# New order numbers for the second part of a three-stage kernel, and three pieces of work placed behind others

## The chip, the cores and the metric

One core of a Trainium2 chip runs the whole program. Its engines are TensorE (PE in the profile; PEld is its loading of weights), VectorE (DVE), ScalarE (ACT), GpSimd (POOL) and SyncE (SP). The metric is the device time of one execution in microseconds (us), a median over runs; less is better.

## The reference

Three stages follow one another; the output of each is the input of the next.

```python
# 1. attention with random features; q, k, v: (8, 8, 576, 64), w_phi: (64, 128)
proj = einsum(x, w_phi); proj -= max(abs(proj))
phi  = concat(exp(proj), exp(-proj))
num / den = phi(q) @ (phi(k)^T v)  /  phi(q) . sum(phi(k))
# 2. 4608 tokens of 512, 8 experts of capacity 576
logits = x @ w_gate
for (token, expert) in descending order of logits:       # greedy
    if token is free and expert has room: assign
out[mask_e] = relu(x[mask_e] @ w1[e]) @ w2[e]             # 512 -> 1024 -> 512
# 3. on all tokens
h = x @ w_in                                              # 512 -> 2048
return (h - tanh(h)) @ w_out                              # 2048 -> 512
```

## The kernel before

The program is in two parts. The first, the attention with its own order numbers `AT`, ends at about 503 us and is not touched. The second is the function `ffn`. It takes the experts one after another, so that a token's whole way (both expert layers, then w_in, the function and w_out) is done while it is on the chip.

All matrices are held as two 16-bit numbers, a high part and the low rest, so each product of two matrices is three matmuls (high by high, high by low, low by high). "Splitting" a matrix is a scaling, a conversion to the high part and a subtraction that leaves the low part.

For expert p the parts are these; lines are those of the kernel before.

- `routing(p)`: the greedy choice. DVE makes integer keys from the logits (L843 multiplies and compares, L880 and L883 arrange, L846 and the last L843, an exclusive or, make the key). Then 16 steps of a search follow, each of which counts keys over three bounds: two counts on DVE (L898), one on ACT (L896), L846 takes ACT's, one small matmul (L902) sums over partitions, L904 compares, and L850 and L843 set the next bounds. The search for expert p+1 runs while expert p is computed; only the first stands alone.
- `xt(p)`: the tokens. POOL issues five indirect gathers (L1161). For expert 0 TensorE transposes them (L1169), for the others a DMA does, after ACT and DVE have split them (L1179, L1180).
- `wprep(p)`: the weights. POOL issues the gathers of w1 and w2 (L1097), ACT sums squares for the scale (L309), L1105 adds them up, and then each of the four pieces is split: w1 of expert 0, and both matrices of experts 2 to 7, by ACT and DVE (L1118, L1119); w2 of expert 0 and both matrices of expert 1 (the table `WPOOL`) by two passes of ACT and a subtraction on POOL (L1114, L1115, L1116).
- `g1(p)`: the first expert layer, 16 tiles of 128 x 288 results with 12 matmuls each (L1190, `mm<-xh,wt`). Each tile is drained by ACT's relu (L1203), copied to the high part (L1204) and its low part is made on POOL (L1205). There are three accumulators `mm` and three buffers `r`.
- `g2(p)`: the second expert layer, 8 tiles of 24 matmuls, drained by ACT (L1216) and DVE (L1217) into `y`. Then `scale_g(p)` finds the scale for what follows (L1233, L1237).
- `batch(p)`: 16 column groups f. For each, 12 matmuls with w_in (L1190, `mm<-gw,win`), then the function h - tanh(h) in pieces on ACT (L1315 to L1318, L1335) and DVE (L1324, L1325, L1327, L1328, L1336), whose result g is a pair of the ring of five, and 12 matmuls with w_out (L1342) that add into four accumulators `po`. At the end of a batch the four are evicted by ACT (L1353) into a ring of two buffers, and POOL scatters each to the output rows (L1357).
- a batch holds 512 of an expert's 576 tokens. The other 64 of each expert are put aside (`rest`) and make a ninth batch at the end of the program, with its own lines for the function (L1311 to L1313, L1321, L1322, L1331 to L1333).

Two things happen once, ahead of expert 0: `split64(1)` splits w_out in 16 chunks (ACT L763 and L764, POOL L765), and `scale_x` finds the scale of the tokens (L1128 to L1137, of which L1130 is the first step that needs data).

The order of instructions is made when the program is built. Each operation of `ffn` is handed to a list scheduler with its engine, an expected duration, the tiles it reads and writes, and a number, its priority (`pri`). The scheduler walks through time and gives each engine the ready operation with the lowest number. So the table `FT` is a table of due times: expert p has `expert`·p, its first layer's tiles come `g1` apart, its batch starts `tb` later with `step` per column group, the product with w_out is `lag` behind the product with w_in of the same group, and `sq`, `th`, `sq2`, `dv`, `dv2` and `gh` are the pieces of the function; `ev` is the evictions' offset from the end of the batch. What the chip sees of this is only the order on each engine; waits on the chip come from the data. An `after=` list, or a key that an operation reads without using its data, also acts on the order only.

## Time and profile before

| what | us |
|---|---|
| median of three runs | 1783.58 |
| the runs | 1783.58, 1779.04, 1784.16 |
| the profiled execution | 1777.59 |
| its span | 1775.8 |
| attention, to the first step of the first search | 503 |
| first matmul of expert 0 | 566.43 |
| last matmul of the program begins its row at | 1755.16 |
| busy in the span: PE, DVE, ACT, POOL | 1638.1, 1333.1, 1270.8, 515.9 |

A row of a timeline is one instruction or several of the same kind in a run: its start, how long it lasted, engine, line, operation, what is written <- what is read, shapes, and count. In square brackets stands how long the engine was idle before it, and whose end ended that. A row of waits has the waiting engine and tile, whom it waited for, the total time, how often, and the longest. PEclk is the granted TensorE clock as a share of full speed: 1.00 is the upper of its two levels, 2.4 GHz, and a stretch between 0.5 and 1.00 has run in part at 1.2 GHz. Names in the trace are those of a memory's first user: `gw` can be the attention's tile or what lies there later, as g of a batch.

### The profile page before, as it was taken

What the parts mean: (1) busy time and instruction counts of PE and PEld (TensorE: products, weight loads), DVE (VectorE), ACT (ScalarE), POOL (GpSimd) and SP (SyncE); (2) the same over time, 40 slices, a digit from 0 to 9 for tenths busy, and PEclk for the clock granted to TensorE, in tenths of its full rate; (3) what the DMA queues carried; (4) which work ended last, traced back from release to release, by engine and by line L of the source; (5) the groups of instructions that cost most, each with busy time, mean ns of one, the idle gap of its engine ahead of it and who ended that gap; (6) DMA issues with size and microseconds to landing.
All of it is one profiled execution on the core that took longest, in us unless ns stands there. A gap on an engine that the chain in (4) does not pass through costs nothing. (4 is left out here: it accounts for less than half of the span.)

```text
span 1775.8 us, 32280 instructions
## 1 busy us (share of the span) xinstructions
PE 1638.1 (92%) x11448; PEld 1066.1 (60%) x11448; DVE 1333.1 (75%) x4118; ACT 1270.8 (72%) x2513; POOL 515.9 (29%) x559
## 2 busy tenths in 40 slices
PE   6899999999935999999999999999999999999995
PEld 5888888888822744754754654664664664564442
DVE  6778888778878499589589689689679548436784
ACT  7787889877775679678678668668758658546653
POOL 3332245423043434432332332322322430210000
PEclk9999999889966999999999999999999999999998
DMA  8778776765503022022022022022113250000000
GB/s 202 171 183 190 185 168 153 160 169 142 140 19 115 11 84 63 28 84 69 25 84 65 25 79 71 28 67 76 32 61 83 63 107 13 25 1 1 18 7 24
DMA packets 230419, 145.95 MB, mean 82 GB/s; under 512 B 166080, under 2 KB 208960, under 8 KB 230256
## 3 DMA queue, kind: packets, MB, share of 16 engines
q1 hardware_dynamic: 214208, 90.25, 22.3%
q0 software_dynamic: 16048, 53.62, 9.4%
q8 instruction: 90, 1.47, 0.3%
q14 instruction: 73, 0.60, 0.1%
HBM read 89.16 MB, written 18.87 MB: 61 GB/s over the span
## 5 line engine op out<-in xcount | busy, mean ns | idle before, releaser
L1342 PE MATMUL po<-wout,gw 128*128 128x512 f16 x1728 | 401.3, 380 | 7.6 <-DVE gw L1336 3.9
L1190 PE MATMUL mm<-xh,wt 128*128 128x288 f16 x3072 | 392.2, 288 | 17.2 <-ACT r L1203 10.9
L1190 PE MATMUL mm<-gw,win 128*128 128x512 f16 x1728 | 397.2, 379 | 5.5 <-DVE gw L1217 3.0
L1190 PEld LDWEIGHTS <-wt 128*128 128x128 f16 x3072 | 296.1, 99 | 103.1 <-issue 17.4
L1342 PEld LDWEIGHTS <-gw 128*128 128x128 f16 x1728 | 164.3, 98 | 205.4 <-DVE gw L1336 11.4
L1190 PEld LDWEIGHTS <-win 128*128 128x128 f16 x1728 | 166.0, 98 | 199.3 <-issue 8.2
L1097 POOL DMA_INDIRECT wt<-moe_w,wrow x96 | 125.8, 1310 | 288.9 <-issue 148.4
L544 PE MATMUL bKV<-vp,kp 128*128 128x96 f32 (+1 forms) x1152 | 173.6, 290 | 3.6 <-ACT kvs L551 3.6
L570 PE MATMUL bN<-kvs,qt 128*128 128x96 f32 (+1 forms) x1152 | 158.1, 285 | 5.1 <-ACT qt L527 3.1
L1205 POOL TENSOR_TENSOR xh<-r,xh 128x288 f16<-128x288 f32 x128 | 95.7, 758 | 215.2 <-ACT xh L1204 214.1
L544 PEld LDWEIGHTS bKV<-vp,kp 128*128 128x128 f32 x1152 | 148.2, 197 | 12.9 <-POOL vp L450 4.2
L570 PEld LDWEIGHTS bN<-kvs,qt 128*128 128x128 f32 x1152 | 144.9, 198 | 8.3 <-ACT qt L527 3.3
L1335 ACT ACTIVATE gw<-s,sc 128x512 f16<-128x512 f32 x128 | 91.9, 718 | 53.4 <-DVE s L1328 46.3
L1315 ACT ACTIVATE u<-mm,sc 128x512 f32<-128x512 f32 x128 | 87.0, 679 | 58.4 <-PE mm L1190 57.4
L1336 DVE SCALAR_TENSOR_TENSOR gw<-s,sc,gw 128x512 f16<-128x512 f32 x128 | 98.1, 766 | 18.9 <-ACT gw L1335 18.4
L1324 DVE SCALAR_TENSOR_TENSOR u<-mm,sc,u 128x512 f32<-128x512 f32 x128 | 94.5, 741 | 20.2 <-ACT t L1316 17.2
L1328 DVE COPY_PREDICATED s<-mk,t 128x512 f32<-128x512 uint16 x144 | 105.5, 733 | 0.9
L1317 ACT ACTIVATE s<-u,cst 128x512 f32<-128x512 f32 x144 | 102.9, 714 | 1.3 <-DVE gw L1336 1.2
L1318 ACT ACTIVATE mk<-u,cst 128x512 f16<-128x512 f32 x144 | 102.4, 711 | 0.0
L1327 DVE SCALAR_TENSOR_TENSOR s<-s,u 128x512 f32<-128x512 f32 x144 | 99.9, 694 | 0.8
L904 DVE TENSOR_SCALAR_CACHE_REDUCE r_nn<-rtp,r_rem 128x7 f32<-128x7 f32 x112 | 24.9, 223 | 96.6 <-PE rtp L902 96.5
L1325 DVE SCALAR_TENSOR_TENSOR t<-mm,sc,t 128x512 f32<-128x512 f32 x128 | 94.7, 740 | 2.5 <-ACT t L1316 2.4
(312 smaller groups left out, 2905.6 us busy)
## 6 DMA issues: line engine op xcount, KB each, us to landing
rawk<-k SPq DMA_DIRECT2D x32, 256.0 KB, 3.5
rawv<-v SPq DMA_DIRECT2D x32, 256.0 KB, 3.5
gw<-moe_w_in SPq DMA_DIRECT2D x32, 256.0 KB, 3.2
gw<-moe_w_out SPq DMA_DIRECT2D x32, 256.0 KB, 3.1
rawq<-q SPq DMA_DIRECT2D x30, 256.0 KB, 3.9
xd<-X SPq DMA_DIRECT2D x32, 192.0 KB, 2.6
xd<-X SPq DMA_DIRECT2D x32, 64.0 KB, 2.4
wt<-moe_w,wrow POOLq DMA_INDIRECT x96, 4.2
```

The source lines that it names most:

```text
L544: mm(o, kp[:, c, a * NF:(a + 1) * NF], r, start=sl == 0 and a == 0, stop=sl == 8 and a == 1, skip_group_check=True)
L570: mm(o, qt[:, a, c], r, start=a == 0, stop=a == 1, skip_group_check=True)
L1097: S.pool(1040, lambda dst=dst, col=col, wf=wf: gp.indirect_dma_start(out=dst, out_offset=None, in_=wf, in_offset=bass.IndirectOffsetOnAxis ...
L1190: nc.tensor.matmul(pt.t[:, 0:un], wt(a, d), xs[hl][:, d, u0:u0 + un], start=d == 0 and a == 0 and hl == 0, stop=d == nb - 1 and a == 1)
L1205: S.pool(700, lambda r=r, f=f, u0=u0, un=un: gp.tensor_tensor(hl[:, f, u0:u0 + un], r, hh[:, f, u0:u0 + un], OP.subtract), [kr, f"h.{f}h{u ...
L1317: S.act(512, lambda u=u, s_=s_: act(s_, u, AF.Square, bias=cst[:, 0:1], scale=PC ** 0.5), [ku, "pa"], [ks], pri=tf + FT["sq2"])
L1318: S.act(512, lambda u=u, mk=mk: act(mk, u, AF.Relu, bias=cst[:, 8:9], scale=1024.0), [ku, "t2"], [km], pri=tf + FT["sq2"])
L1325: S.dve_s(512, lambda t=t, pt=pt, sc=sc: v.scalar_tensor_tensor(t, pt.t, sc[:, 0:1], t, op0=OP.mult, op1=OP.subtract), [pt, ksc, kt], [kt])
L1327: S.dve(512, lambda s_=s_, u=u: v.scalar_tensor_tensor(s_, s_, PC * PB, u, op0=OP.add, op1=OP.mult), [ks, ku], [ks], port=True)
L1328: S.dve(512, lambda s_=s_, mk=mk, t=t: v.copy_predicated(s_, mk.bitcast(U16), t), [ks, km, kt], [ks], port=True)
L1336: S.dve_s(512, lambda s_=s_, g=g, sc=sc: v.scalar_tensor_tensor(g[:, 1], s_, sc[:, 2:3], g[:, 0], op0=OP.mult, op1=OP.subtract), [ks, kgr ...
L1342: nc.tensor.matmul(outs[t].t, g[:, a, 128 * t:128 * t + 128], self.wout[:, w, f, :], start=f == 0 and k_ == 0, stop=f == 15 and k_ == 2)
```

## The change

The numbers of `FT` are new: 16 of its 24 entries. Three pieces of work get something to stand behind in the order. w_out's split (`split64(1)`) and the first step of the tokens' scale (L1130) are listed as readers of "r.key", which the search's key operation writes. The gathers of w2 for expert 0 come after the first tokens' gathers, which `xt` now collects in `came`. No instruction is added or removed, and all lines from L1154 on move down by up to three.

```diff
-FT = {'expert': 136.0, 'step': 5.3, 'lag': 11.0, 'route': 5.0, 'xt': -30.0, 'g1': 3.0, 'g2': 24.0, 'g2s': 6.0, 'sg': 49.0, 'tb': 50.0, 'w1': 30.0, 'w2': 40.0, 'rest': 10.0, 'ev': 8.0, 'tb8': 85.0, 'sq': 1.0, 'th': 1.2, 'sq2': 1.1, 'dv': 1.0, 'dv2': 2.0, 'gh': 3.0, 'h': 0.0, 'late': 1.2, 'room': 0.0}
+FT = {'expert': 136.0, 'step': 1.8, 'lag': 12.4, 'route': 5.0, 'xt': -30.0, 'g1': 2.5, 'g2': 21.1, 'g2s': 5.2, 'sg': 46.4, 'tb': 53.6, 'w1': 30.0, 'w2': 40.0, 'rest': 27.4, 'ev': -1.8, 'tb8': 64.6, 'sq': 1.0, 'th': 25.4, 'sq2': 3.4, 'dv': 20.9, 'dv2': 2.0, 'gh': 3.4, 'h': -3.3, 'late': 0.6, 'room': 0.0}
...
-    def split64(self, which, cw):
+    def split64(self, which, cw, after=()):
...
-            S.act(cw, lambda f=f, sc=sc: act(f, f, AF.Copy, scale=sc), [f"S64.{which}"], kf)
+            S.act(cw, lambda f=f, sc=sc: act(f, f, AF.Copy, scale=sc), [f"S64.{which}", *after], kf)
...
-            tt(JE, key, VT.bitcast(I32), key, OP.bitwise_xor, "VT wide", "wide")
+            tt(JE, key, VT.bitcast(I32), key, OP.bitwise_xor, "VT wide", "wide key")
...
-                            [kr], [kr_[c], kr_[c] + "h"], lat=4500)
+                            [kr], [kr_[c], kr_[c] + "h"], lat=4500, after=came if p == 0 and n else ())
...
-            S.dve(48, lambda: v.tensor_reduce(nx, self.ssx, axis=AX.X, op=OP.add), [], ["nx"])
+            S.dve(48, lambda: v.tensor_reduce(nx, self.ssx, axis=AX.X, op=OP.add), ["r.key"], ["nx"])
...
+        came = []
...
+            came.clear()
...
-                S.pool(1040, lambda x=x, m=m, t=t: gp.indirect_dma_start(
+                g = S.pool(1040, lambda x=x, m=m, t=t: gp.indirect_dma_start(
...
+                came.append(g)
...
-        split += self.split64(1, CW)
+        split += self.split64(1, CW, ["r.key"])
```

What the order becomes, at three places. First, on POOL at the start of the second part: L765 is w_out's split, L884 clears a tile of the search, L1097 are weight gathers (128x1024 of w1, 128x512 of w2), L1161 the tokens' gathers. Before:

```order
154 L765 TENSOR_TENSOR wout<-gw,wout 128x512 x2
155 L884 MEMSET r_V 128x288
156 L765 TENSOR_TENSOR wout<-gw,wout 128x512 x14
157 L1097 DMA wt<-moe_w,wrow_6308 128x1024 x4
158 L1097 DMA wt<-moe_w,wrow_6308 128x512 x3
159 L1161 DMA xg_6221<-xd,idx_6301 128x512
160 L1161 DMA xg_6222<-xd,idx_6301 128x512
161 L1161 DMA u_6227<-xd,idx_6301 128x512
162 L1161 DMA u_6228<-xd,idx_6301 128x512
163 L1161 DMA u_6229<-xd,idx_6301 128x512
164 L1097 DMA wt<-moe_w,wrow_6308 128x512 x3
165 L884 MEMSET r_V 128x288
```

and of the change:

```order
154 L884 MEMSET r_V 128x288
155 L765 TENSOR_TENSOR wout<-gw,wout 128x512 x16
156 L1097 DMA wt<-moe_w,wrow_6308 128x1024 x4
157 L1163 DMA xg_6221<-xd,idx_6301 128x512
158 L1163 DMA xg_6222<-xd,idx_6301 128x512
159 L1163 DMA u_6227<-xd,idx_6301 128x512
160 L1163 DMA u_6228<-xd,idx_6301 128x512
161 L1163 DMA u_6229<-xd,idx_6301 128x512
162 L884 MEMSET r_V 128x288
163 L1097 DMA wt<-moe_w,wrow_6308 128x512 x7
```

The clearing L884 of the search comes ahead of all of w_out's split, and the five token gathers (now L1163) come ahead of all seven of w2's gathers here, where three stood in front of them.

Second, DVE in the same place, from the multiplication L843 to the counts: L1130, L1131, L1133 and L1135 are the tokens' scale, L898 is the first count. Before:

```order
1422 L843 TENSOR_TENSOR r_wide<-r_wide,few 128x288
1423 L1131 TENSOR_REDUCE cst<-nx 128x1
1424 L877 TENSOR_REDUCE r_cm<-r_wide 128x36
1425 L1133 TENSOR_SCALAR s_6232<-cst 128x128
1426 L843 TENSOR_TENSOR r_mask<-few,r_cm 128x288
1427 L779 COPY rtp<-cand 128x54
1428 L880 COPY_PREDICATED r_V<-r_mask,L 128x288
1429 L1135 TENSOR_REDUCE cst<-po_6256 128x1
1430 L883 STREAM_TRANSPOSE r_VT<-r_V 128x288
1431 L846 TENSOR_SCALAR r_wide<-r_VT 128x288
1432 L843 TENSOR_TENSOR r_wide<-r_VT,r_wide 128x288
1433 L898 TENSOR_SCALAR r_buf,r_cnt<-r_wide,few 128x288 x2
```

and of the change:

```order
1421 L843 TENSOR_TENSOR r_wide<-r_wide,few 128x288
1422 L877 TENSOR_REDUCE r_cm<-r_wide 128x36
1423 L843 TENSOR_TENSOR r_mask<-few,r_cm 128x288
1424 L779 COPY rtp<-cand 128x54
1425 L880 COPY_PREDICATED r_V<-r_mask,L 128x288
1426 L883 STREAM_TRANSPOSE r_VT<-r_V 128x288
1427 L846 TENSOR_SCALAR r_wide<-r_VT 128x288
1428 L843 TENSOR_TENSOR r_wide<-r_VT,r_wide 128x288
1429 L898 TENSOR_SCALAR r_buf,r_cnt<-r_wide,few 128x288
1430 L1130 TENSOR_REDUCE nx<-ssx 128x12
1431 L898 TENSOR_SCALAR r_buf,r_cnt<-r_wide,few 128x288
1432 L846 TENSOR_SCALAR r_cnt<-r_ac 128x1
```

The four instructions of the scale leave the chain between the multiplication and the first count; the first of them, L1130, now stands between the counts.

Third, ACT and expert 1's w2 (L1114, L1115). Before, they stand in the batch of expert 0, among the function's pieces:

```order
933 L1315 ACTIVATE u_6228<-mm_6254,sc_6236 128x512
934 L1114 ACTIVATE wt<-wt,sc_6237 128x1024 x2
935 L1115 ACTIVATE wt<-wt 128x1024
936 L1114 ACTIVATE wt<-wt,sc_6237 128x1024 x2
937 L1179 ACTIVATE xs_6223<-xg_6222,cst 128x512
938 L1115 ACTIVATE wt<-wt 128x1024
939 L1335 ACTIVATE gw<-s_6233,sc_6236 128x512
940 L1317 ACTIVATE s_6232<-u_6228,cst 128x512
941 L1318 ACTIVATE mk_6235<-u_6228,cst 128x512
942 L1316 ACTIVATE t_6231<-mm_6254,sc_6236 128x512
943 L1115 ACTIVATE wt<-wt 128x1024
```

and of the change, in expert 1's first layer, where L1206 and L1207 are the drains of the tiles (before L1203 and L1204):

```order
989 L1206 ACTIVATE r_6226<-mm_6255 128x288
990 L1207 ACTIVATE xh<-r_6226 128x288
991 L1114 ACTIVATE wt<-wt,sc_6237 128x1024 x2
992 L1115 ACTIVATE wt<-wt 128x1024
993 L1114 ACTIVATE wt<-wt,sc_6237 128x1024 x2
994 L896 ACTIVATE r_jk,r_ac<-wo,r_K 128x288
995 L1115 ACTIVATE wt<-wt 128x1024
996 L1206 ACTIVATE r_6224<-mm_6253 128x288
997 L1206 ACTIVATE r_6225<-mm_6254 128x288
```

Two passes each on four pieces, with a count of the search (L896) between, now stand as one run between the drain of the accumulator mm_6255 and that of mm_6253.

And the end of TensorE's program, of 18629 rows in both, where every second row loads weights. The last product with w_in before:

```order
18554 L1190 MATMUL mm_6254<-gw,win 128x512
18555 L1190 LDWEIGHTS win
18556 L1190 MATMUL mm_6254<-gw,win 128x512
18557 L1342 LDWEIGHTS gw
18558 L1342 MATMUL po_6258<-wout,gw 128x512
```

and of the change:

```order
18458 L1193 MATMUL mm_6254<-gw,win 128x512
18459 L1193 LDWEIGHTS win
18460 L1193 MATMUL mm_6254<-gw,win 128x512
18461 L1345 LDWEIGHTS gw
18462 L1345 MATMUL po_6258<-wout,gw 128x512
```

Between the last product with w_in and the end stand 36 matmuls with w_out before (three column groups) and 84 now (seven).

## Rows read from the trace of the kernel before

**Rows 1.** Windows, core 0: busy us (count) per engine, PEclk, DMA share, GB/s.

```profile
800.00:920.00 120.00, 118.57 (x737) 70.36 (x736) 94.45 (x307) 84.80 (x165) 34.08 (x35) 1.00 0.19 57
```

**Rows 2.** Waits of PE, 500 to 800 us: total us, times, longest us.

```profile
PE rtp L902 <- DVE r_cnt L846: 18.8, 11, 3.0
PE mm L1190 <- ACT r L1203: 5.0, 2, 4.3
...
PE mm L1190 <- DVE u L1324: 2.0, 1, 2.0
PE mm L1190 <- DVE wt L1119: 1.8, 2, 0.9
...
PE po L1342 <- DVE gw L1336: 1.5, 1, 1.5
```

**Rows 3.** Waits of PE, 800 to 1776 us.

```profile
PE mm L1190 <- ACT r L1203: 5.9, 8, 2.0
PE mm L1190 <- DVE gw L1217: 4.4, 5, 2.4
PE po L1342 <- DVE gw L1336: 2.4, 7, 0.7
PE po L1342 <- ACT gw L1332: 2.2, 2, 1.7
...
PE po L1342 <- ACT gw L1353: 0.6, 1, 0.6
```

**Rows 4.** Timeline, DVE and POOL, 503 to 511 us.

```profile
503.56 0.46 DVE L843 TENSOR_TENSOR r_wide<-L,r_m 128x288 f32<-128x288 f32 x1
...
504.06 1.28 DVE L843 TENSOR_TENSOR r_wide<-r_wide,few 128x288 f32<-128x288 f32 x1
...
505.75 0.69 DVE L1133 TENSOR_SCALAR s<-cst 128x128 f32<-128x128 f32 x1
...
507.50 0.28 DVE L1135 TENSOR_REDUCE cst<-po 128x1 f32<-128x128 f32 x1
...
508.52 4.76 POOL L765 TENSOR_TENSOR wout<-gw,wout 128x512 f16<-128x512 f32 x4
...
508.76 1.28 DVE L843 TENSOR_TENSOR r_wide<-r_VT,r_wide 128x288 int32<-128x288 int32 x1
...
510.19 0.51 DVE L898 TENSOR_SCALAR_CACHE_REDUCE r_buf<-r_wide,few 128x288 bf16<-128x288 int16 x1
```

**Rows 5.** Timeline, DVE, one step of the first search.

```profile
518.55 0.16 DVE L846 TENSOR_SCALAR r_cnt<-r_ac 128x1 f16<-128x1 f32 x1 [0.36 <-ACT r_jk L896]
```

**Rows 6.** Timeline, PE, the first tokens' transposes.

```profile
561.08 1.97 PE L1169 MATMUL po<-identf,xg 128*128 128x128 f32 x8 [1.11 <-DMA xg<-xd,idx]
```

**Rows 7.** Timeline, ACT and PE, first layer of expert 0.

```profile
589.31 2.19 ACT L1114 ACTIVATE wt<-wt,sc 128x1024 f32<-128x1024 f32 x2
...
595.89 0.68 ACT L1203 ACTIVATE r<-mm 128x288 f32<-128x288 f32 x2
...
597.08 5.37 PE L1190 MATMUL mm<-xh,wt 128*128 128x288 f16 x27
```

**Rows 8.** Windows after two of the holes.

```profile
596.00:602.00 6.00, 5.67 (x29) 3.79 (x29) 1.48 (x9) 3.92 (x11) 5.94 (x5) 0.58 0.01 3
...
1552.00:1556.00 4.00, 3.75 (x20) 2.49 (x20) 0.73 (x4) 2.98 (x8) 3.76 (x6) 0.66 0.06 23
```

**Rows 9.** Timeline, POOL, DVE and PE, batch of expert 0.

```profile
703.34 2.13 POOL L1116 TENSOR_TENSOR wt<-wt 128x1024 f16<-128x1024 f32 x1 [1.50 <-ACT wt L1115]
...
703.91 2.11 DVE L1336 SCALAR_TENSOR_TENSOR gw<-s,sc,gw 128x512 f16<-128x512 f32 x1 [0.81 <-ACT gw L1335]
...
706.08 3.77 PE L1342 MATMUL po<-wout,gw 128*128 128x512 f16 x10 [1.54 <-DVE gw L1336]
```

**Rows 10.** Timeline, ACT and PE, start of a later expert's first layer.

```profile
1551.78 0.41 ACT L1203 ACTIVATE r<-mm 128x288 f32<-128x288 f32 x1 [3.43 <-POOL xh L1205]
...
1552.24 34.17 PE L1190 MATMUL mm<-xh,wt 128*128 128x288 f16 x264 [1.99 <-ACT r L1203]
```

## The prediction

> **What bounds the kernel now.** I read the stages first, then TensorE's waits, then the timelines of the places where a wait was long. The first half, the attention, is the same text in both kernels, so I count nothing there. In the second half the steady stage is TensorE's: between 800 and 920 us it is busy for 118.57 of 120 us at a granted clock of 1.00, with DVE at 94 us, ACT at 85 us and POOL at 34 us [rows 1]. A new order can't shorten that matmul work; it can only close holes. So I list the holes. Before 800 us TensorE waits most for the first search's counts (18.8 us in 11 waits, when it has nothing else to do), once for 4.3 us for ACT's drain of a first-layer tile (L1203), for 2.0 us for DVE's L1324, for 1.5 us for DVE's L1336 [rows 2]. From 800 us to the end it waits 5.9 us in eight pieces for L1203, 4.4 us in five for L1217, 2.4 us in seven for L1336 and 2.8 us in three for ACT pieces named L1332 and L1353 [rows 3]. Everything that the change can win after the front is in these lists, and in the matmuls that follow a hole: after one, the granted clock is lower for a while (0.58 in 596 to 602 us, 0.66 in 1552 to 1556 us, which is half speed for part of it) [rows 8].
>
> A full-speed first-layer matmul starts every 34.17 / 264 = 0.129 us [rows 10], so the 27 that took 5.37 us after the 4.3 us hole [rows 7] lost 5.37 − 27 × 0.129 = 1.9 us more to the clock; the 3.75 us of TensorE in 1552 to 1556 us for 20 of them lost 3.75 − 2.58 = 1.2 us [rows 8].
>
> **Part 1, the front: the three new orderings.** The split of w_out waits for the keys, and so does the first step of the tokens' scale. What they leave is DVE's chain up to the first count. In it, the multiplication L843 on 128x288 took 1.28 us where the comparison of the same form beside it took 0.46 us; the xor took 1.28 us as well, with POOL's L765 running from 508.52 us [rows 4]. Two such at 0.82 us are 1.64 us. The scale's L1133 (0.69 us) and L1135 (0.28 us) go out of the chain, and so do L1130 and L1131, which I put at not more than 0.28 us each; they overlap at their ends, so I take 1.0 us for the four [rows 4]. That makes the keys 2.6 us earlier, since the chain has no other wait in it that the split would have covered.
>
> Against it stands that the split does not vanish: ACT's and POOL's pieces lie between the search's steps, and ACT counts in each step (L896). Before, one step shows what a late ACT costs: DVE idle for 0.36 us before L846 [rows 5]. All 16 steps late would cost 5.8 us, none late nothing; the split's front is some chunks of 16, so I take three late steps, 1.1 us. The gathers of w2 for expert 0 now stand behind the first tokens' gathers on POOL's queue (the order shows three of the seven passed). TensorE's first transposes waited 1.11 us for these tokens [rows 6]: that is the most it can give. But behind the tokens the first matmuls waited for DVE's L1119 (1.8 us in two waits [rows 2]), which the gathers of w1 feed, and these stay in front; so I take nothing for it. w2's data are wanted only when expert 0's first layer is done, which covers their later issue. If that cover is gone, it costs up to the three gathers' issue time, which no row here shows apart, and I leave it to the range. Part 1: −2.6 + 1.1 = −1.5 us, between −3.7 (the tokens in full, no late step) and +3.2 (16 late steps).
>
> **Part 2, the new numbers: expert 1's w2.** The order shows the largest move here. Before, the conversion of expert 1's w2 (ACT L1114 and L1115, POOL L1116) stands among the elementwise work of the first second-layer stage; now ACT does four L1114, two L1115 and a count in one piece between two drains of expert 1's first layer.
>
> What goes: in that second-layer stage POOL's L1116 (2.13 us) stands beside DVE's L1336, which took 2.11 us, and TensorE idled for 1.54 us and then took 3.77 us for 10 matmuls [rows 9]. By columns a 512-wide matmul is 0.129 × 512 / 288 = 0.23 us, so 1.5 us of these 3.77 are the clock. With the 2.0 us wait for L1324 of the same stage [rows 2] this is 2.0 + 1.5 + 1.5 = 5.0 us. L1324's wait lies behind DVE work slowed in the same way by w1's L1116, which now stand behind the token gathers. I take all of it: −5.0 us, between −5.0 and 0 (they collide with other two-input DVE work).
>
> What comes: expert 0's first layer already has such a piece of ACT: four L1114, two L1115 and a count from 589.31 to 595.89 us, and it is this piece that TensorE waited 4.3 us for, with 1.9 us of slow clock behind it [rows 2, 7]. Behind ACT's piece stand the drains L1206, and for these stand TensorE's three tiles. Expert 1's stage has the same three tiles and the same piece of work, so I price it the same: +4.3 + 1.9 = +6.2 us, between 0 (the data are late, and the conversion falls apart between drains) and +8 (POOL's four L1116 at 2.13 us also hold back the low halves, L1208).
>
> By the Trainium skill ("SBUF — State Buffer", section "Who interferes with whom") a DVE instruction with two SBUF inputs and a GpSimd instruction that reads SBUF exclude each other, and the later one waits for the whole of the first. The trace agrees with it in size: 1.28 against 0.46 us and 2.11 us beside a POOL instruction of 2.13 us [rows 4, 9]. By that rule the moved L1116 could each stop the next search in expert 1's first layer for up to 2.13 us, an estimate of +8.5 us if TensorE waited for every one; by the rows it waits there for ACT, not DVE [rows 2], and I leave the sum as it is.
>
> **Part 3, the end.** The ninth batch (L1311 to L1333) has the waits for L1332 and L1353, 2.2 + 0.6 us [rows 3]. Now the second product lags further behind the first in TensorE's order, and seven groups of it stand behind the last product with w_in, where three stood. The first matmuls of each group have their g ready. Price −2.8 us, between −2.8 and 0. The longer end itself costs nothing, as the matmul count is the same; the evictions behind it are the same four.
>
> **Part 4, the steady stage.** 'lag' over 'step' goes from 11 / 5.3 = 2 to 12.4 / 1.8 = 7 groups, so the product with w_out asks for its g later: the waits for L1336, 2.4 us in seven [rows 3], go. The waits for L1217 are the hop from first to second layer (the last tile's drain and DVE's step must end before the next product), and no order of the same parts fills them unless the second product of another expert stands there, which it doesn't: 0. What is late next are the drains where the evictions of a second-layer stage meet the next first layer; I leave these as they are. So −2.4 us, between −12.7 (all three lists' waits of L1203, L1217 and L1336) and the rival below.
>
> **Sum.** −1.5 − 5.0 + 6.2 − 2.8 − 2.4 = −5.5 us. The profiled execution took 1777.59 us (span 1775.8 and 1.8 around it), so it would give 1772.1. The median of the three runs is 6.0 us higher, 1783.58; against that, 1783.6 − 5.5 = 1778.1, and I say 1778.0.
>
> **Rivals.**
> 1. *The evictions hold the next first layer.* The numbers ask for a second-layer stage's eviction right at its end, so ACT meets L1353's ring of two buffers just when the drains of the next first layer are due. Before, this is seen once in full: ACT idles 3.43 us before L1203, TensorE 1.99 us [rows 10], and 1.2 us of clock come after it. It decides from the point where ACT is held for longer than TensorE's three tiles last, 3 × 12 × 0.129 = 4.6 us. At each of seven changes of expert this is 7 × 3.2 = 22.4 us; 5.9 + 1.2 = 7.1 of that are lost already [rows 3, 8], so +15.3: 1778 + 15.3 = 1793 us, slower. For it speaks that the product with w_out now ends all at once; against it that TensorE then has this product to do while ACT waits. Chance 0.17.
> 2. *The holes close.* The deeper lag leaves TensorE work at every change of expert, and the waits for L1203 and L1217 go too: 5.9 + 1.2 + 4.4 = 11.5 us more, 1766.5 us. For it: the lag of seven groups. Against: a product of one expert can't begin before that expert's hop. Chance 0.20.
> 3. *Only the places change.* The small waits move to other lines and the end stays, so parts 3 and 4 are nothing; −1.5 − 5.0 + 6.2 = −0.3: 1783.3 us, no change. For it: DVE and ACT are 79% and 71% busy in the steady stage [rows 1], and waits of 0.3 us reappear anywhere. Chance 0.22.
>
> **How the numbers follow.** The forecast has 0.41; its own range is 1774 to 1782. What a measurement of this kernel can tell from no change is 0.3%, 5.4 us, so the forecast is at this border: of its 0.41, 0.26 falls under faster and 0.15 under same, since the new hole of part 2 has a price from nothing to 8. Rival 2 is all faster. Rival 3 gives 0.18 same, 0.02 faster and 0.02 slower; rival 1 gives 0.15 slower, 0.02 same. Faster 0.26 + 0.20 + 0.02 = 0.48, same 0.15 + 0.18 + 0.02 = 0.35, slower 0.15 + 0.02 = 0.17. The range takes in rival 2 with a little more (1765) and of rival 1 the cases with up to half of the seven holes (to 1790).
>
> **What would show it.** Part 1: the first L898 count starts at 508 us rather than 510.19 [rows 4], no L843 above 0.6 us before it, and the first transposes with less than 1.11 us idle. Part 2: no wait of TensorE above 1 us around 680 to 710 us, and one of some 4 us in expert 1's first layer (around 720 to 745 us) that ends with a drain, with a granted clock near 0.6 behind it; without it the time is near 1772. Part 3: no wait for ACT of over 0.5 us in the last 30 us. Part 4: the wait list from 800 us without DVE's g, and L1217's five waits unchanged. Wrong it would be if the list from 800 us grew by over 10 us of waits for drains (rival 1) or shrank to under 5 us (rival 2).

## The result: slower by 0.8%

The changed kernel takes 1795.97 us, median of 13 runs (1789.32 to 1812.65), against 1783.58 us for the kernel before (13 runs, 1777.03 to 1790.07). The ratio is 1.008, with a 95% interval from 1.0051 to 1.0109. 1778.0 us was forecast, in a range from 1765 to 1790: both the direction and the range were wrong. The rival in which the evictions hold up the next first layer had been given a chance of 0.17 and 1793 us. Its place, its sign and nearly its time came, but what holds the first layer is another thing than it said.

The profiled execution has a span of 1787.6 us, 11.8 more than before. The attention, which is the same in both kernels, ended later in this execution (the search's first row, L868, starts at 506.0 us against 503.1), so the stages are counted from that row on. "Batch p" is the first product of batch p with w_in, from TensorE's timeline; all times in us.

| profile | first count (L898) | batch 0 | 0 to 1 | 1 to 7 | 7 to the last matmul | sum |
|---|---|---|---|---|---|---|
| before | 7.1 | 123.3 | 141.5 | 819.5 | 170.8 | 1255.2 |
| the change | 5.7 | 122.8 | 147.7 | 827.0 | 166.4 | 1263.9 |

The front and the end gain, 0.5 and 4.4 us. Expert 1's stage loses 6.2 us, and the six changes of expert behind it lose 7.5 us. Each row is one execution, and of the 12.4 us between the medians the table holds 8.7. The column of batch 0 varies between executions: it lies between 122.6 and 126.6 us in the eight profiles of this document with the old order of the front, so the 0.5 us says little by itself. TensorE's waits of the changed kernel, first from 500 to 800 us, then from 800 us to the end (total us, times, longest):

```profile
PE rtp L902 <- DVE r_cnt L846: 22.6, 12, 2.7
...
PE mm L1193 <- ACT r L1206: 3.6, 4, 1.2
PE mm L1193 <- POOL wt L1116: 3.5, 1, 3.5
```

```profile
PE mm L1193 <- ACT r L1206: 18.4, 14, 2.6
PE mm L1193 <- DVE gw L1220: 2.2, 5, 0.5
PE rtp L902 <- DVE r_cnt L846: 1.9, 4, 0.5
```

The second list stands against [rows 3]: the waits for w_out's products are gone, as forecast, and those for the hop from the first expert layer to the second (L1217, now L1220) have halved, but the waits for the drains (L1203, now L1206) went from 5.9 us in eight to 18.4 us in fourteen. Two waits at the search's small matmuls have grown by less (L902 1.9 us and, not printed here, L988 1.5 us). One change of expert, on POOL, then ACT, then TensorE (timelines of the changed kernel):

```profile
1138.94 0.98 POOL L1360 DMA_INDIRECT out<-gw,idx  x1 [2.64 <-ACT r L1206]
1143.57 0.97 POOL L1360 DMA_INDIRECT out<-gw,idx  x1 [3.64 <-ACT gw L1356]
1147.15 0.97 POOL L1360 DMA_INDIRECT out<-gw,idx  x1 [2.61 <-issue]
1148.14 1.42 POOL L1208 TENSOR_TENSOR xh<-r,xh 128x288 f16<-128x288 f32 x2
```

```profile
1142.86 0.69 ACT L1356 ACTIVATE gw<-po,sc 128x512 f32<-128x512 f32 x1 [2.86 <-DMA out<-gw,idx]
...
1148.91 0.41 ACT L1206 ACTIVATE r<-mm 128x288 f32<-128x288 f32 x1 [3.06 <-POOL xh L1208]
```

```profile
1144.23 3.30 PE L1193 MATMUL mm<-xh,wt 128*128 128x288 f16 x24 [1.91 <-ACT r L1206]
1149.37 0.90 PE L1193 MATMUL mm<-xh,wt 128*128 128x288 f16 x6 [1.84 <-ACT r L1206]
```

The scatters of one batch are 3.6 us and more apart, though POOL is busy with each for only 1.0 us. ACT waits twice: first for a scatter to land, since an output buffer must come free, and 6 us later for POOL, since L1208 stands behind the last scatter and the three `r` buffers are full. TensorE has three tiles of work for each of these, and then stops.

The order on POOL shows how often this can happen. At seven changes of expert there are three places each between two scatters. In the kernel before nothing stands between them at 6 of these 21 places, in the change at 18.

### The profile page after: what moved, and what is told of

Its sections match the earlier page's. It is cut to its first block, busy times and chain, and to the rows that moved or that the text cites. A ratio compares the mean times of both kernels' runs of the same rounds, so it can differ in the third digit from the quotient of the medians.

```text
span 1787.6 us, 32384 instructions
## 1 busy us (share of the span) xinstructions
PE 1640.6 (92%) x11447; PEld 1068.9 (60%) x11448; DVE 1332.7 (75%) x4118; ACT 1264.8 (71%) x2513; POOL 486.7 (27%) x559
## 5 line engine op out<-in xcount | busy, mean ns | idle before, releaser
L1193 PE MATMUL mm<-xh,wt 128*128 128x288 f16 x3072 | 398.5, 289 | 28.2 <-ACT r L1206 22.1
L1193 PE MATMUL mm<-gw,win 128*128 128x512 f16 x1728 | 391.5, 379 | 4.5 <-DVE gw L1220 2.7
L1345 PE MATMUL po<-wout,gw 128*128 128x512 f16 x1728 | 390.0, 379 | 0.0
L570 PE MATMUL bN<-kvs,qt 128*128 128x96 f32 (+1 forms) x1152 | 161.7, 289 | 4.2 <-ACT qt L527 2.2
L1097 POOL DMA_INDIRECT wt<-moe_w,wrow x96 | 102.3, 1065 | 167.5 <-DVE wt L1119 55.3
L1360 POOL DMA_INDIRECT out<-gw,idx x32 | 33.2, 1036 | 416.7 <-ACT gw L1356 368.2
L1208 POOL TENSOR_TENSOR xh<-r,xh 128x288 f16<-128x288 f32 x128 | 97.7, 777 | 41.0 <-ACT xh L1207 40.0
L1328 DVE SCALAR_TENSOR_TENSOR t<-mm,sc,t 128x512 f32<-128x512 f32 x128 | 95.3, 745 | 17.0 <-ACT t L1319 16.8
L1327 DVE SCALAR_TENSOR_TENSOR u<-mm,sc,u 128x512 f32<-128x512 f32 x128 | 95.4, 745 | 14.2 <-ACT mk L1321 9.6
```

The source lines that it names most:

```text
L570: mm(o, qt[:, a, c], r, start=a == 0, stop=a == 1, skip_group_check=True)
L1097: S.pool(1040, lambda dst=dst, col=col, wf=wf: gp.indirect_dma_start(out=dst, out_offset=None, in_=wf, in_offset=bass.IndirectOffsetOnAxis ...
L1193: nc.tensor.matmul(pt.t[:, 0:un], wt(a, d), xs[hl][:, d, u0:u0 + un], start=d == 0 and a == 0 and hl == 0, stop=d == nb - 1 and a == 1)
L1208: S.pool(700, lambda r=r, f=f, u0=u0, un=un: gp.tensor_tensor(hl[:, f, u0:u0 + un], r, hh[:, f, u0:u0 + un], OP.subtract), [kr, f"h.{f}h{u ...
L1327: S.dve_s(512, lambda u=u, pt=pt, sc=sc: v.scalar_tensor_tensor(u, pt.t, sc[:, 0:1], u, op0=OP.mult, op1=OP.mult), [pt, ksc, ku], [ku])
L1345: nc.tensor.matmul(outs[t].t, g[:, a, 128 * t:128 * t + 128], self.wout[:, w, f, :], start=f == 0 and k_ == 0, stop=f == 15 and k_ == 2)
```

## The experiments

Each ratio is to the kernel before, with its 95% interval; the stage columns are those above.

| run | median us | ratio | first count | batch 0 | 0 to 1 | 1 to 7 | 7 to end |
|---|---|---|---|---|---|---|---|
| e1 numbers alone | 1810.48 | 1.0131 (1.0085 to 1.0177) | 7.1 | 125.3 | 147.3 | 843.0 | 166.4 |
| e2 orderings alone | 1781.20 | 0.9982 (0.9953 to 1.0010) | 5.2 | 121.2 | 142.6 | 817.5 | 170.8 |
| e3 change, plain writes | 1766.31 | 0.9890 (0.9841 to 0.9940) | 5.3 | 122.7 | 142.3 | 814.6 | 166.4 |
| e4 change, four buffers | 1837.82 | 1.0285 (1.0233 to 1.0338) | 5.5 | 123.0 | 154.5 | 870.9 | 167.4 |
| e5 change, chain known | 1781.55 | 0.9991 (0.9974 to 1.0008) | 5.4 | 124.3 | 142.4 | 819.3 | 166.4 |
| e6 orderings, chain known | 1767.90 | 0.9921 (0.9877 to 0.9966) | 5.2 | 123.2 | 140.3 | 807.8 | 170.8 |
| e7 before, plain writes | 1762.48 | 0.9894 (0.9850 to 0.9938) | 7.1 | 126.6 | 140.5 | 807.6 | 170.8 |
| e8 change, ev 60 | 1795.75 | 1.0078 (1.0047 to 1.0109) | 5.4 | 123.1 | 148.9 | 831.3 | 166.4 |
| e9 e5 with late 1.2 | 1772.72 | 0.9941 (0.9917 to 0.9964) | 5.3 | 123.7 | 145.6 | 811.0 | 166.4 |
| e10 batch's numbers | 1794.94 | 1.0089 (1.0055 to 1.0122) | 7.1 | 122.6 | 148.2 | 834.6 | 166.4 |
| e11 the other numbers | 1791.80 | 1.0051 (1.0021 to 1.0081) | 7.1 | 122.6 | 139.5 | 826.3 | 175.7 |
| e12 e6, w2 of expert 0 | 1766.47 | 0.9912 (0.9878 to 0.9946) | 5.8 | 116.8 | 143.0 | 809.9 | 170.8 |
| e13 before, late 0.6 | 1815.12 | 1.0194 (1.0134 to 1.0254) | 7.1 | 125.9 | 145.4 | 847.3 | 170.9 |
| e14 change, late 1.2 | 1821.20 | 1.0199 (1.0144 to 1.0254) | 5.2 | 123.6 | 147.9 | 861.9 | 166.4 |
| e15 e12, last batch | 1758.89 | 0.9854 (0.9812 to 0.9895) | 5.4 | 115.6 | 143.1 | 807.1 | 166.9 |
| e16 e13, quarter gathers | 1817.58 | 1.0190 (1.0137 to 1.0243) | 7.1 | 125.8 | 145.1 | 847.6 | 170.8 |
| e17 change, quarter gathers | 1810.26 | 1.0134 (1.0080 to 1.0188) | 5.4 | 125.5 | 149.1 | 844.5 | 166.4 |
| e18 before, quarter gathers | 1781.39 | 0.9976 (0.9950 to 1.0003) | 7.1 | 126.0 | 141.5 | 815.4 | 170.8 |

### e1 and e2: the two halves of the change

e1 is the kernel before with the new `FT` line, e2 the change with the old one.

> The new numbers alone, without the three new orderings. Theory A (the new numbers put all four evictions of a batch at the start of the next expert's first layer, and ACT and POOL stand still there): ratio to the kernel before 1.007, as the whole change, TensorE's waits for the drains after 800 us about 18 us against 5.9 before. Theory B (the loss is at the front and in expert 1's weights, from the orderings): ratio 1.000 to 1.002.

> The three new orderings alone, with the old numbers. Theory A: ratio 0.999 to 1.001, waits for drains after 800 us about 6 us as before, first counts 1.4 us earlier after the search's first step but nothing left of it at the first full-rate matmul. Theory B: ratio 1.004 to 1.008.

The orderings alone are no loss, and the first count comes 1.9 us earlier; the numbers alone are slower than the whole change. So theory B falls. The size of e1 (1.0131) is more than theory A gave, and its waits for drains from 800 us on (16.9 us) are no longer than the change's: what it loses beyond the change isn't shown to come from the scatters.

### e3, e4 and e7: what makes a scatter wait

```diff
 e3 and e7
-gp.indirect_dma_start(out=self.out, out_offset=bass.IndirectOffsetOnAxis(ap=idx, axis=0), in_=ob, in_offset=None)
+gp.dma_start(out=self.out[at:at + 128, :], in_=ob)      # at = 512 * b + 128 * t
 e4
-rob = Ring(..., [ob0, ob1])
+rob = Ring(..., [ob0, ob1] + ru.t[0:2], ["ob.0", "ob.1"] + ru.k[0:2])
```

> The whole change, with the same order on TensorE, ACT and POOL, but the 36 output writes go to consecutive rows by plain DMAs instead of to the tokens' rows (the output is in another order): so no write waits for the one before it. Theory A1 (each scatter waits on POOL for the DMA of the scatter before it, some 3.6 us each, and the drains' low halves stand behind it): waits for drains after 800 us fall from 18 us to under 6, ratio to before 0.995 to 1.000. Theory A2 (two output buffers hold ACT): the waits fall a little, a buffer is still one DMA of over 2 us, to some 10 us, ratio 1.003. Theory B: no difference from the change, 1.007.

> The whole change with four output buffers instead of two (the others are two of the function's u tiles, which are free then). Theory A1: ACT no longer waits for a DMA at its evictions, but POOL still waits for each scatter before the next and ACT then waits for POOL: waits for drains after 800 us stay at 12 to 18 us, ratio 1.004 to 1.007. Theory A2: they fall to some 4 us, ratio 0.998 to 1.000. Theory B: 1.007.

> The kernel before, with the output writes to consecutive rows by plain DMAs (the output is in another order). It prices the chain of scatters in the order before. Theory A1: the waits for drains after 800 us (5.9 us and 1.2 us of slow clock behind one) go, ratio 0.995 to 0.997; that leaves the new numbers some 5 us better than the old ones where no scatter waits (the change gave 1766.3 so). Rival (plain DMAs are shorter on all engines, and that is what made the change faster): ratio 0.990.

The built program shows the chain: a scatter may write any row of `out`, so each one waits for the DMA of the one before (DMASW are the semaphores of POOL's DMAs). The second and third scatter of a batch in the change, and the same two in e3, where the rows are known to be apart:

```
312 L1360 DMA out<-gw,idx_6302 4608x512 [waits DMASW5_49,DMASW4_49,Activation_49]
313 L1360 DMA out<-gw,idx_6302 4608x512 [waits DMASW6_49,DMASW5_49,Activation_49]

311 L1360 DMA out<-gw 128x512 [waits DMASW5_49,Activation_49]
312 L1360 DMA out<-gw 128x512 [waits DMASW6_49,Activation_49]
```

Without the chain and with the same order of instructions, the waits for drains from 800 us on are gone from the list, and e3 is 1.1% faster than the kernel before and, by the two ratios, 1.9% faster than the change. Four buffers alone made it far worse, which theory A1 had not priced: now ACT does all four evictions at once, and nothing stands between two scatters at any of the 21 places. POOL, ACT and TensorE in e4:

```profile
1020.64 1.99 POOL L1360 DMA_INDIRECT out<-gw,idx  x1 [2.49 <-ACT r L1206]
1025.10 0.97 POOL L1360 DMA_INDIRECT out<-u,idx  x1 [2.48 <-issue]
1028.70 0.97 POOL L1360 DMA_INDIRECT out<-u,idx  x1 [2.63 <-issue]
1029.70 2.10 POOL L1208 TENSOR_TENSOR xh<-r,xh 128x288 f16<-128x288 f32 x3
...
1030.47 0.41 ACT L1206 ACTIVATE r<-mm 128x288 f32<-128x288 f32 x1 [6.42 <-POOL xh L1208]
...
1030.93 2.32 PE L1193 MATMUL mm<-xh,wt 128*128 128x288 f16 x9 [3.94 <-ACT r L1206]
```

So what ACT and TensorE wait for at this change of expert is POOL's queue, and more buffers don't help (A2 falls). The two added buffers are tiles that the function uses too, and e4 does not tell what that costs.

e7 came out as its rival had it, 0.9894, and not as theory A1 (0.995 to 0.997). Plain writes are worth 1.1% in the old order and 1.9% in the new, and in total the two are then equally fast (0.9894 and 0.9890). Two things limit what this shows. First, part of both gains is at the end: behind the last matmul the kernel before goes on for 17.6 us, e3 and e7 for 11.0 us, since there too a scatter waits for the one before it (POOL of the kernel before):

```profile
1760.73 0.97 POOL L1357 DMA_INDIRECT out<-gw,idxm  x1 [2.49 <-DMA out<-gw,idxm]
1764.18 0.97 POOL L1357 DMA_INDIRECT out<-gw,idxm  x1 [2.48 <-DMA out<-gw,idxm]
```

Second, the totals are equal and the stages are not. In expert 1's stage the chain is what the change lost: without it 142.3 us against 140.5, with it 147.7 against 141.5. From batch 1 to 7 e3 still takes 7.0 us more than e7 (814.6 against 807.6), nearly what the change takes more than the kernel before. The waits for drains are not there; e3 has others in their place, 5.5 us at L988 and one of 2.9 us for which the list names nobody. So the chain makes the waits for drains, but that it is the whole loss of this stage is not shown. A plain write also needs no indices, and how much of the 1.1% is that and not the chain, these two runs don't tell.

### e5, e6 and e8: the order, with the chain as it is

```diff
 e5 (on the change) and e6 (on e2)
-S.pool(1040, lambda ob=ob, it=it: scatter(ob, it), [ko] + kit, [], lat=2500)
+S.pool(1040, lambda ob=ob, it=it: scatter(ob, it), [ko] + kit, ["out"], lat=2500)
 e8 (on the change, one entry of the FT line)
-'ev': -1.8
+'ev': 60.0
```

> The whole change, and the list scheduler is told that a scatter writes 'out', so that it counts the scatter before it (its issue and 2.5 us of flight) and puts other POOL work in between; on the chip no wait is added or taken away. Theory A1 (a scatter stands on POOL until the one before has landed, and the drains' low halves stand behind it): waits for drains after 800 us from 18 us to some 5 us, ratio to the kernel before 0.990 to 0.997. Rival A3 (it is the flight itself: two output buffers let no eviction end earlier, whatever stands between): waits stay over 12 us, ratio over 1.003.

> The three orderings with the old numbers, and the scheduler told of the chain of scatters. Theory A1: the old order already had drains between most scatters, so little is left: waits for drains after 800 us from 6.2 to some 3 us, ratio to before 0.994 to 0.998. Rival: no change against the orderings alone, 0.998.

> The whole change, with the evictions due 60 after the batch's last group in place of -1.8, so that drains of the next expert go first on ACT. Theory A1: POOL's order gets drains between the scatters, by luck of the numbers rather than by knowledge of the chain: waits for drains after 800 us fall from 18 us to 6 to 12 us, ratio to before 0.998 to 1.004. Rival A3: no change, 1.007.

One word tells the scheduler what the chip does anyway. In e5 POOL gets L1208 between the scatters, and the waits for drains fall from 18.4 to 1.1 us (POOL's timeline at a change of expert, then TensorE's waits from 800 us):

```profile
1146.42 1.85 POOL L1360 DMA_INDIRECT out<-gw,idx  x1 [2.64 <-ACT r L1206]
1148.30 0.74 POOL L1208 TENSOR_TENSOR xh<-r,xh 128x288 f16<-128x288 f32 x1
1150.90 0.99 POOL L1360 DMA_INDIRECT out<-gw,idx  x1 [1.86 <-ACT gw L1356]
1151.93 3.11 POOL L1208 TENSOR_TENSOR xh<-r,xh 128x288 f16<-128x288 f32 x3
1155.20 0.98 POOL L1360 DMA_INDIRECT out<-gw,idx  x1 [0.16 <-issue]
```

```profile
PE mm L1193 <- DVE t L1328: 5.6, 7, 2.5
PE mm L1193 <- DVE gw L1220: 2.0, 4, 0.6
PE mm L1193 <- DVE u L1327: 1.8, 2, 1.3
...
PE mm L1193 <- ACT r L1206: 1.1, 2, 0.8
```

e5 is 0.9% faster than the change: the two stages that lost are back at 142.4 and 819.3 us. It is not faster than the kernel before. e6, with the old numbers, is: 0.9921, where theory A1 asked for 0.994 to 0.998; other work stands between two scatters at all 21 places, and its list from 800 us has no wait for a drain at all. So with the chain known to both, the new numbers still cost 0.7% (e5 against e6), 11.5 us of it from batch 1 to 7, and other waits have grown there: 7.4 us for DVE's L1327 and L1328 in e5.

e8 missed: TensorE's waits for drains fall to 4.2 us, more than expected, but the total stays, 1.0078, as its rival had it. TensorE now waits elsewhere, 6.3 us for L1327 and L1328 and 6.9 us at the search's L988. A later due time is no substitute for the dependence, and shorter waits for drains alone do not make the kernel faster.

### e10 and e11: which numbers

e10 has `step`, `lag`, `ev`, `th`, `sq2`, `dv`, `gh` of the new table in the kernel before, e11 has the rest.

> The kernel before with seven new numbers, those of the batch: step, lag, ev, th, sq2, dv, gh. Theory A1 (step 1.8 makes the whole batch due 56 earlier, evictions with it, so that all four scatters stand together): waits for drains after 800 us over 14 us, ratio 1.006 to 1.013. Rival (the other numbers set it): ratio 1.000.

> The kernel before with the other new numbers: g1, g2, g2s, sg, tb, rest, tb8, late (and h, which no line reads). Theory A1: waits for drains after 800 us near 6 to 9 us, ratio 0.999 to 1.004, of which Theory C asks for something above 1.000 from waits at the search's small matmuls. Rival of e10: 1.007 or more.

Both halves lose. e10 has the drains' waits (16.7 us from 800 us on) and the end's gain, as theory A1 said. e11 has 8.6 us of them, a longer end, and a ratio just above its expectation. So the waits for drains come from the batch's numbers in the main, and the loss from both halves.

### e9, e13, e14: a theory that fell

What was left of the loss in e5 looked like TensorE waiting at the search's small matmuls (11.0 us behind 590 us), and of the new numbers `late` sets those.

> The change with the scheduler told of the chain of scatters, and 'late' back from 0.6 to 1.2 (the room that the search's small matmuls get on TensorE behind the moment when their data are due). Theory C (what is left of the loss then, some 7 us against the old numbers, is TensorE waiting at the search's small matmuls and at what DVE does for them): waits of L902, L988, L1105 and of the product with w_in for DVE's L1327 and L1328 after 566 us fall from 27 us to under 15, ratio to the kernel before 0.993 to 0.996. Rival D (it comes from the batch's own numbers, which put the function's pieces behind the product): no change from 0.999.

> The kernel before with one number changed, 'late' from 1.2 to 0.6. Theory C: TensorE's waits at L902, L988, L1105 and the like after 566 us grow from 1 us to about 10, ratio to the kernel before 1.003 to 1.006. Rival D (it takes the other numbers too): 1.000.

> The change with 'late' back at 1.2 and nothing else. Theory C and A1 together: the waits at the search's small matmuls go from 10 to about 1 us, the drains' waits stay near 20 us, ratio to before 1.002 to 1.005. Rival D: 1.008, as the change.

e9 came out as expected: no such wait, 0.9941, which is within 0.2% of e6. e13 was slower by more than it should have been, and e14, which should have gained, lost 1.2% more: the waits at the search's matmuls are 10.0 us there too. So `late` is no cause by itself; it moves instructions about, and what that does hangs on the rest of the order. The trace of e13 shows one of the waits. DVE:

```profile
785.58 0.43 DVE L981 TENSOR_TENSOR wo<-c,r_pos 128x512 f16<-128x512 f16 x1 [7.33 <-remote]
```

ACT stands still for 3.35 us beside it. It happens while POOL issues ten weight gathers one after another (771.2 to 783.7 us). "Remote" means that a semaphore ended the wait and the view names no sender, and the trace itself says more. L981 waits for TensorE's semaphore, because the matmuls of L988 must have read `wo` before it is written again. By their rows these matmuls and the next two that signal ended at 778.04, 778.79 and 779.46 us, with three products of 512 columns between each two. The semaphore's updates stand at 785.56, 785.64 and 785.70 us. They are too close together for the products to have run between them, so TensorE's work was done and its signals came 6 to 7.5 us late (the ends of matmuls are modelled, so this is a reading). All 32 such idle times of DVE and ACT over 0.9 us behind 590 us, in all the runs, are waits for TensorE's semaphore.

### e16 to e18: is it the gathers' bytes?

```diff
+m = 32 if p > 1 else 128
-out=dst, ... ap=row[:, col:col + 1]
+out=dst[0:m], ... ap=row[0:m, col:col + 1]       # and [0:m] in L309, L1118, L1119
```

> e13 ('late' 0.6 in the kernel before) with the weight gathers of experts 2 to 7 and what reads them on 32 partitions instead of 128 (a quarter of the bytes; the other weights are left from an earlier expert, so the output is not the reference's). Theory F: the idle times of ACT and DVE with releaser 'remote' after 700 us (11 us on ACT, 7 us on DVE in e13) go, ratio to the kernel before from 1.019 to 1.005 to 1.010. Theory C (TensorE waits at the search's matmuls because 'late' puts them too early): they stay, 1.015 to 1.020.

> The change with the same quarter gathers. Theory A1 with F: the change's profile shows one such idle time of 2.4 us and scatters' waits of 20 us; the first goes, the second stays: ratio to before 1.004 to 1.008. If the gathers' packets also slow the scatters: 1.000 or less.

> The kernel before with the same quarter gathers, the measure for the other two. Its trace shows no idle time of this kind over 0.9 us. Theory F: ratio to before 0.997 to 1.000. If smaller gathers help by themselves: under 0.995.

Theory F falls as it stood. The DMA queue of the gathers while they are issued (packets, MB, share of 16 engines; 771 to 786 us of e13, 779 to 794 us of e16), and DVE in e16:

```profile
q0 software_dynamic: 1054, 3.67, 72.6%
```

```profile
q0 software_dynamic: 384, 0.92, 20.8%
```

```profile
794.10 0.42 DVE L981 TENSOR_TENSOR wo<-c,r_pos 128x512 f16<-128x512 f16 x1 [7.33 <-remote]
```

A quarter of the bytes, the same 7.33 us and the same ratio (1.0190 against 1.0194). So the gathers' traffic isn't what holds up TensorE's signals. Nor is it the loading of code at these two places: no packet of the instruction queues moves in the two windows. What stays open is what does hold them up, and why one order meets it and another doesn't: the kernel before, the change and e9 have no "remote" idle time above 0.9 us behind 590 us, e5 and e17 three each, e13 seven. (The one of 2.4 us that e17's expectation gives to the change, on L1119, has another ending on its row, "issue".) e18 came out as expected, so smaller gathers by themselves change nothing. e17's ratio is above its expectation and above the change's, 1.0134 against 1.0080, though their intervals overlap; no theory here explains it.

### e12 and e15: a faster version

```diff
 e12 (on e6)
-WPOOL = {(0, 1), (1, 0), (1, 1)}
+WPOOL = {(1, 0), (1, 1)}
 e15 (on e12), in batch(b)
+num = {**FT, "step": 1.8, "lag": 12.4, "th": 25.4, "sq2": 3.4, "dv": 20.9, "gh": 3.4} if mix else FT
-tf = T0 + FT["step"] * f
+tf = T0 + num["step"] * f       # and so for the other five
```

> The best so far (three orderings, old numbers, the scheduler told of the chain), with w2 of expert 0 split by ACT and DVE (L1118, L1119) as the later experts' are, in place of two ACT passes and POOL. If ACT's run of 7 us in the first layer of expert 0 is what TensorE waits 2.6 to 4.3 us for there, with 1.8 us of clock behind it: ratio to before 0.989 to 0.991, against 0.992 without. Rival: DVE, which is in the search there, delays the counts by as much: 0.992 to 0.994.

> e12 with the batch's new numbers (step, lag, th, sq2, dv, gh) for the last, mixed batch alone. If the end's gain is its own (166.4 us from the last batch's first product to the end of TensorE, against 170.8): 4 us less than e12, ratio to before 0.987 to 0.990. Rival (the end's gain comes from 'tb8' and needs the whole table): 0.991, as e12.

e12 gains 6 us up to batch 0 (123.2 to 116.8), gives 2.7 of them back in the stage behind, and is no more than level with e6 in total, just above its expectation. e15 has the end's gain (170.8 to 166.9 us) with the rest of the old table: 1758.89 us, 0.9854 (0.9812 to 0.9895), the fastest version that computes the reference, 1.5% under the kernel before and 2% under the change.

## Why the prediction was wrong, point by point

**Part 1, the front, −1.5 us: the net was right, by luck.** The key's multiplication and its exclusive or took 0.46 us each where they had taken 1.28 [rows 4], and the first count came 1.4 us earlier after L868. That is less than the 2.6 counted for the chain; 0.8 us of what is missing is a new wait, DVE's for the table of candidates. By the Trainium skill ("SBUF — State Buffer", section "Who interferes with whom") a VectorE instruction with two SBUF inputs contends with a GpSimd instruction that reads SBUF. The trace agrees: w_out's split (L765) is gone from beside the two, POOL has no row of it from 506 to 513 us, and both are short.

```profile
507.01 0.46 DVE L843 TENSOR_TENSOR r_wide<-r_wide,few 128x288 f32<-128x288 f32 x1
...
509.23 0.22 DVE L779 COPY rtp<-cand 128x54 f32<-128x54 f32 x1 [0.78 <-DMA cand<-cand]
...
511.11 0.46 DVE L843 TENSOR_TENSOR r_wide<-r_VT,r_wide 128x288 int32<-128x288 int32 x1
511.72 0.51 DVE L898 TENSOR_SCALAR_CACHE_REDUCE r_buf<-r_wide,few 128x288 bf16<-128x288 int16 x1
```

At batch 0 the change's profile is 0.5 us ahead and e2's 2.1. Over all the profiles with the old split of expert 0's w2, the mean of that column is 124.8 us with the old orderings (eight runs) and 123.3 with the new (ten, 121.2 to 125.5): −1.5 us. So the net agrees though its first term was 1.2 us too large; the 1.1 us that were charged against it are not measured by themselves.

**Part 2, expert 1's w2, +1.2 us net: the net was right without the scatters, the cause of what came was not.** The stalls of expert 0's batch [rows 9] went, as forecast, and ACT's run came (TensorE waited 2.75 us for a count and 0.88 us for a drain behind it, not the 4.3 us of [rows 2]):

```profile
744.51 0.17 PE L902 MATMUL rtp<-r_cnt,c 128*128 128x7 f16 x1 [2.75 <-DVE r_cnt L846]
745.56 3.48 PE L1193 MATMUL mm<-xh,wt 128*128 128x288 f16 x18 [0.88 <-ACT r L1206]
```

In e3, without the chain, the stage takes 142.3 us, 0.8 more than before, near the net of 1.2; the −5.0 and the +6.2 are not measured one by one. In the change it takes 147.7, because a scatter that waits stands ahead of the last L1116 of w1, for which the prediction had no term. POOL, then TensorE, and the clock behind it:

```profile
718.74 0.98 POOL L1360 DMA_INDIRECT out<-gw,idx  x1 [2.59 <-issue]
719.74 2.13 POOL L1116 TENSOR_TENSOR wt<-wt 128x1024 f16<-128x1024 f32 x1
```

```profile
721.93 1.12 PE L1193 MATMUL mm<-xh,wt 128*128 128x288 f16 x7 [3.47 <-POOL wt L1116]
...
722.92 4.67 PE L1193 MATMUL mm<-xh,wt 128*128 128x288 f16 x24
```

```profile
722.00:728.00 6.00, 6.00 (x38) 4.22 (x39) 1.82 (x12) 2.82 (x9) 2.73 (x3) 0.72 0.27 87
```

After the 3.47 us, 24 matmuls took 4.67 us, 1.6 more than at the full rate of [rows 10], with a granted clock of 0.72 in this stretch. Together that is 5.1 of the 5.4 us between the change and e3.

**Part 3, the end, −2.8 us: right in kind, −4.4 in size.** It appears in every run with the batch's new numbers (166.4 us against 170.8), and e15 has 3.9 us of it by the last batch's numbers alone. TensorE's idle time in this stretch went from 3.7 to 0.5 us, so 3.2 us are waits that the longer queue of products hid; where the other 1.2 come from is not shown.

**Part 4, the steady stage, −2.4 us: this step failed.** Its sentence "what is late next are the drains where the evictions of a second-layer stage meet the next first layer; I leave these as they are" is the error. From batch 1 to batch 7 the change loses 7.5 us where 2.4 were to be won. The waits for g went, and 12.5 us of waits for drains, which the prediction had put at nothing, came. That is over the 10 us that it had named as the sign of being wrong. By the table the evictions of a batch were due at 50 + 16 × 5.3 + 8 = 142.8 after their expert's start, behind the next expert's at 136; now they are due at 53.6 + 16 × 1.8 − 1.8 = 80.6, so they outrank the next expert's drains on ACT and POOL. The rival had the place, the sign and nearly the time (1793 us for 1796), but not the holder: it spoke of a ring of two buffers, and e4 shows that more buffers make it worse. That the time fits is partly luck, since 6.2 us of the loss came in expert 1's stage, at L1116, which the rival does not have. The row that could have told was [rows 10]: ACT's 3.43 us there ended with POOL's L1205, not with a DMA that frees a buffer. The prediction does not say what POOL did in these 3.43 us. It is this (POOL of the kernel before), a scatter that waits for the one before it:

```profile
1550.02 0.97 POOL L1357 DMA_INDIRECT out<-gw,idx  x1 [2.50 <-DMA out<-gw,idx]
```

The chance of 0.17 came from weighing one such hole, and not from asking how the new due times order the scatters at all seven changes of expert.

What the waits for drains rest on is shown by the two ways of taking them away (e3, e5) and by the count of places with nothing between two scatters: 6 before, 18 in the change, 21 in e4, none in e6. What stays open is the rest of this stage's loss. With plain writes the new numbers are still 7.0 us behind the old ones from batch 1 to 7, with the chain known 11.5 us, and the waits are then at the search's small matmuls and for DVE's pieces of the function. The prediction has no term for the number `late`, which in e5 and e9 is worth 0.5%.

## What to carry to other kernels

When an order puts pieces next to each other that wait for one another on the chip, and the scheduler does not know it, the queues behind them can stop. Give the scheduler the dependence that the program has anyway (here one key, 0.9% on the change, 0.6% on the orderings). Follow a wait to the engine behind it, and on that engine to what it was doing then; a wait for a buffer may be a wait for a queue. A wait that is taken away need not shorten the kernel, as e8 shows; compare the stages, and not only the list. And the single numbers of such a table had no effect of their own here: the same number, moved the same way, was a gain of 0.5% where the scheduler knew the chain and a loss of 1.2% where it did not.

## What the runs showed of the hardware

A scatter of 128 rows of 2 KB occupies POOL for 1.0 us, and one that must wait for it starts 3.45 us after it where nothing else holds it (the last four of the kernel before), and 3.4 to 4.7 us at most of the other places. TensorE's signals can reach the other engines 6 to 7.5 us after the end that its rows give, while GpSimd issues gathers one after another; this stood at the same instruction and lasted as long when the gathers' bytes were cut to a quarter (e13, e16). And the first part of the program, identical in all these kernels, ended anywhere between 501.8 and 520.8 us in the profiles: a difference of a few us between two totals is only read safely from a point behind it.
